# T5-bias attention with a mixture of adapters on one Trainium2 core: edge factors, last tokens' v and score tiles in another order

## The chip, the cores and the metric

The kernel runs on one core of one Trainium2 chip. The core has five engines with an instruction queue each: PE (TensorE, matrix multiply into PSUM), DVE (VectorE), ACT (ScalarE), POOL (GpSimd, which here works on SBUF alone) and SP (which issues nearly all DMAs). The metric is the device time of one execution in microseconds (us), the median of several runs. One execution was also recorded by the hardware profiler; the lines shown come from that one.

## The reference

Attention over 8 batches, 8 heads, 576 tokens and head size 64, with a bias that depends on the distance of two tokens (T5 buckets), then for each token the two best of 8 low-rank adapters are added:

```python
scores = q @ k.T / sqrt(D) + bias_table[bucket(|i - j|)]     # per batch and head
attn = softmax(scores);  x = attn @ v                        # x: 4608 tokens x 512
logits = x @ w_gate                                          # 8 experts, the top 2 per token
w = softmax of the top 2
out = x + sum over the top 2 of w * ((x @ A[e]) @ B[e])
```

All distances of 128 and more share one bucket, so only near pairs of tokens need a bias of their own.

## The kernel before, in words

A unit u is one batch and one pair of heads: 32 units, four for each batch. Tokens 0 to 511 of a batch are the main part, in four key tiles of 128 keys, and tokens 512 to 575 are the last tokens. All of the program is written out by hand in one order (`tc.manual_schedule()`); each engine executes its instructions in the order in which the Python code issues them, and waits on semaphores for the data and buffers that it needs.

For one unit, in the order of the main loop (`for u in range(2, NU - 2)`, before.py's main loop):

- `prep` lets POOL cast q and k of a later unit (L139); `load` issues DMAs on SP for unit u+4.
- `keys(u, c)` for three key tiles: PE writes scores of two heads, 128 keys by 512 queries, into a score tile (L436), adds the bias of near pairs by further matmuls (L441), and ACT takes the exp (L445). `KO` is the order of the four key tiles. In this text the first, second and third keys are these three calls, and the fourth comes further down.
- `step(u - 1, 0)`: the first values of the unit before. It may begin with `moe_d`, in which PE multiplies with the adapters' second factor (L627) and DVE adds x (L304) into an output tile, then PE multiplies probabilities with v (L524 for main keys, L532 for the last tokens' v as keys, L541 and L543 for the last tokens as queries) and, for a finished tile of x, with the gates and adapters' first factor (L571). DVE takes the reciprocal of the sums (L563), normalises (L564), copies z (L576) and its largest values (L577); when a group is complete, POOL does the gating's first four operations (L587 to L593).
- `edge_l(u)` on POOL (L505) and `edge_t(u)` on DVE (L510) multiply the edge probabilities of unit u with their bias factors, in place. An edge is a score between a last token and a main token. These probabilities are wanted by the values of unit u, one stage later.
- `prep_late` lets POOL cast v of unit u+1 (L135), and in some stages q and k of last tokens (L147).
- the fourth keys of u; then `turn`: PE transposes q and k of unit u+2 and tiles of x or gates into a score tile (L379, L377), and DVE copies it to SBUF (L381). In seven stages (`tcorner`: u = 4, 7, 11, 15, 19, 23, 27) the same tile also takes the corner scores of a batch, last tokens against last tokens, whose exp (L386) ACT takes only after the exp of the next unit's edges.
- `edges(u + 1)`: PE writes the edge scores of the next unit (L495, L498), ACT takes their exp (L500).
- `step(u - 1, 1)`: the second values of the unit before, with DVE's reciprocal, normalisation and, at times, z.
- in seven stages (`tv`) `cast_tail` casts the last tokens' v of a batch (L150): POOL the lower half, DVE the upper half. In some stages the gating's second part (`moe_w`), and behind corners POOL multiplies the corner probabilities with their factor (L484).

Score tiles, 128 partitions by two banks of PSUM, come from three pools in turn (`score_tile`). A stage uses six: first, second, third and fourth keys, the turned tile and the next unit's edges. So the second keys of u use the tile of the turned tile of u-1, the third keys that of the edges of u, and the edges of u+1 that of the third keys of u. A tile can be written again when its reader (ACT's exp or DVE's copy) is done. The values go to another pair of PSUM banks, which `moe_d` uses as well.

After the loop the last two units are done with keys in halves, and the last tiles' gates and adapters follow in banks that take the place of the score tiles (`fin`, with `s0` as the number of the pool that would be next).

Of the kernel before, what the change touches and what calls it, by code (L numbers as in the profile page):

```python
# [2 lines left out]

# [1 line left out]

# [22 lines left out]
def _ap(t, offset, dims):  # L28

    return bass.AP(tensor=t.tensor, offset=t.offset + offset, ap=[list(t.ap[0])] + dims)  # L30
# [8 lines left out]
def kernel(  # L39
# [12 lines left out]
    B, H, S, D = q.shape  # L52
# [26 lines left out]
    scx = ExitStack()  # L79
    scps = [scx.enter_context(tc.tile_pool(name=f"sc{i}_ps", bufs=1, space=bass.MemoryType.PSUM))  # L80
            for i in range(3)]
    turns = count()

    def score_tile(name, shape=(128, 2, SM), dt=FP32):
        return scps[next(turns) % 3].tile(list(shape), dt, name=name, tag="sc")

    KO = (0, 2, 1, 3)
    units = [(b, hp) for b in range(B) for hp in range(HP)]
# [42 lines left out]
    def cast(u, nm, eng):  # L131
        s = stage[(u, nm)].rearrange("p h (c d) -> p h c d", c=4)
        if nm == "v":
            t = vts[u % NV]
            eng.tensor_copy(t[:, :, :, :D].rearrange("p c h d -> p h c d"), s)  # L135
        else:
            t = qkp.tile([128, 4, 2, D], BF16, name=f"{nm}n", tag=f"{nm}n")
            copy = eng.copy if eng is nc.scalar else eng.tensor_copy
            copy(t.rearrange("p c h d -> p h c d"), s)  # L139
            nat[(u, nm)] = t  # L140

    def cast_tail(b, nm, eng, g0=0, g1=HP):
        if nm == "qk":
            if g0 == 0:
                nat[(b, nm)] = stt.tile([128, H, D], BF16, name="qkb", tag="qkb")
            part = slice(2 * g0, 2 * g1)
            eng.tensor_copy(nat[(b, nm)][:, part], tstage[(b, nm)][:, part])  # L147
            return
        for f, e in enumerate((eng, nc.vector)):
            e.tensor_copy(tvs[b % 2][f * 64:f * 64 + 64, :, f, :D], tstage[(b, nm)])  # L150
# [64 lines left out]
    def turned(h):  # L215
        return anti[h * 64:h * 64 + 64, 64 - 64 * h:128 - 64 * h]
# [122 lines left out]
    def tile_of(b, i):  # L339
        if (b, i) not in tiles:  # L340
            tiles[(b, i)] = tail_tile(b) if i == 4 else main_tile(b, i // 2, i % 2)
        return tiles[(b, i)]
# [87 lines left out]
    def keys(u, c):  # L430
        b, hp = units[u]
        qT, kT = qkT[u][:, 0, :], qkT[u][:, 1, :]
        sc = score_tile("sc")
        g, e = c // 2, c % 2
        for rows, prt, h, f in QUADS:
            nc.tensor.matmul(sc[prt, h, :],  # L436
                             lhsT=kT[rows, c * 128 + f * 64:c * 128 + f * 64 + 64],
                             rhs=qT[rows, :], start=True, stop=False, skip_group_check=True)
        for rows, prt, h, f in QUADS:
            p0, n, y0 = BAND[g][f]  # L440
            nc.tensor.matmul(_ap(sc[prt, h, :], p0, [[256, 2], [128, 2], [1, n]]), lhsT=turned(h),  # L441
                             rhs=_ap(Wt[rows, hp, :], 2 * y0 + (GP if e else 1),
                                     [[1, 2], [1 - GP if e else GP, 2], [2, n]]),
                             start=False, stop=True, skip_group_check=True)
        nc.scalar.activation(probs[u][0][:, c, :, :], sc, ACT.Exp, scale=scale)  # L445
# [61 lines left out]
    def edge_t(u, eng=nc.vector):  # L507
        hp = units[u][1]
        e = _ap(probs[u][1], 64 + 128, [[SM, 2], [1, 128]])
        eng.tensor_tensor(e, e, ET[:, hp], op=ALU.mult)  # L510
# [35 lines left out]
    def values(u, j):  # L546
        pv = mp.tile([128, 512], FP32, name="pv", tag="mm")
        pv_main(u, pv, j, range(4))
        pv_last(u, pv, j)
        pv_tail(u, pv, j)  # L550
        return pv
# [9 lines left out]
    def normalise(u, j, pv):  # L561
        b, hp, rc = outputs(u)
        nc.vector.reciprocal(rc[:, j, :5], _ap(pv, D, [[W1, 5]]))  # L563
        nc.vector.tensor_tensor(xs[b][:, j, hp], _ap(pv, 0, [[W1, 5], [1, D]]),  # L564
                                _ap(rc, 6 * j, [[1, 5], [0, D]]), op=ALU.mult)
# [3 lines left out]
    def moe_z(t, pv, o=ZO, cs=range(HP), first=False):  # L569
        for c in cs:  # L570
            nc.tensor.matmul(pv[:, o:o + ER + E], lhsT=t.xT[c], rhs=AW[:, c, :], start=first and c == cs[0],  # L571
                             stop=(c == HP - 1), skip_group_check=True)

    def moe_zc(t, pv, o=ZO):
        g, k = t.group, t.k
        nc.vector.tensor_copy(g.z[:, k, :], pv[:, o:o + ER + E])  # L576
        nc.vector.max(g.top[:, k, :], g.z[:, k, ER:])  # L577
        g.left -= 1
        if not g.left:
            moe_s(g)  # L580
# [28 lines left out]
    def moe_t(t, pv, o=ZO):  # L609
        ps = pv[:, o:o + 64].bitcast(BF16)  # L610
        nc.tensor.transpose(ps, t.group.zt[:, t.k, :, :].rearrange("p e r -> p (e r)"), ident)
        return ps

    def moe_tc(t, ps):
        t.zT = ms.tile([128, 128], BF16, name="zT", tag="zT", bufs=6)
        nc.vector.tensor_copy(t.zT, ps)
# [6 lines left out]
    def moe_d(t):  # L623
        dl = mp.tile([128, Dm], FP32, name="dl", tag="mm")
        if t.quarter:
            x_first(t, dl)
        nc.tensor.matmul(dl, lhsT=t.zT, rhs=Bc, start=not t.quarter, stop=True, skip_group_check=t.quarter)  # L627
        ot = ms.tile([128, Dm], FP32, name="ot", tag="ot", bufs=8)
        if t.quarter:
            nc.vector.tensor_copy(ot, dl)  # L630
        else:
            t.add(ot, dl)
        t.store(ot)

    def step(u, j, ds=(), z=None, zt=None):
        for t in ds:
            moe_d(tile_of(*t))
        pv = values(u, j)
        if z:
            moe_z(tile_of(*z), pv)  # L640
        if zt:
            ps = moe_t(tile_of(*zt), pv)
        normalise(u, j, pv)
        if z:
            moe_zc(tile_of(*z), pv)
        if zt:
            moe_tc(tile_of(*zt), ps)
# [90 lines left out]
    tturn = {3 if c == 1 else 6 if c == 2 else 4 * c - 4: c for c in range(1, B)}  # L738
    tload = {max(4 * c - 6, 3): c for c in range(2, B)}
    tq = {w - 1: c for w, c in tturn.items() if c != 2}  # L740
    tv = {4 if c == 1 else 6 if c == 2 else 4 * c - 3: c for c in range(1, B)}

    tcorner = {4 if c == 1 else 4 * c - 1: c for c in range(1, B)}
    pxs = {}

    def prep(u):
        for x in (u + 2, u + 3)[:1 + (u in wq)]:
            if x < NU and (x, "q") not in nat and x not in qkT:
                for nm in ("q", "k"):
                    cast(x, nm, nc.gpsimd)  # L750
        if u == 6:
            cast_tail(2, "qk", nc.gpsimd)

    def prep_late(u):
        if u + 1 < NU:
            cast(u + 1, "v", nc.gpsimd)
        if u in tq:
            cast_tail(tq[u], "qk", nc.gpsimd)

    za, zb, da, db, ta, tb, xt, wq = ({} for _ in range(8))  # L760
# [59 lines left out]
    for u in range(2, NU - 2):  # L820
        b, hp = units[u]
        prep(u)
        if u + 4 < NU:
            load(u + 4)
        if u == 2:
            load_tail(1, "v")
        if u in tload:
            load_tail(tload[u])
        for c in KO[u == 2:3]:
            keys(u, c)  # L830
        if u == 4:
            weights_turn(0)
        zs = za.pop(u, [None])
        step(u - 1, 0, da.pop(u, []), z=zs[0], zt=ta.pop(u, [None])[0])
        edge_l(u)
        edge_t(u)
        prep_late(u)
        if u == 3:
            weights_cast()
        keys(u, KO[3])  # L840
        if u == 4:
            weights_turn(1)
        items = []
        if u + 2 < NU:
            items.append(qk_item(u + 2))
        if u in tturn:
            items.append(tl_item(tturn[u]))
        for fn, bb, i in xt.pop(u, []):
            items.append(fn(tile_for(bb, i)))
        def next_edges():  # L850
            open_probs(u + 1)
            edges(u + 1)

        behind = u in tturn and tturn[u] == units[u + 1][0]
        turn(items, corner=tcorner.get(u), after=None if behind else next_edges)
        zs = zb.pop(u, [None])
        step(u - 1, 1, db.pop(u, []), z=zs[0], zt=tb.pop(u, [None])[0])
        if behind:
            next_edges()
        if u in tv:  # L860
            cast_tail(tv[u], "v", nc.gpsimd)
        for bb, i in wq.pop(u, []):
            moe_w(groups[(bb, i)])
        if u in tcorner:
            corners_bias(tcorner[u], pxs.pop(tcorner[u]))
# [104 lines left out]
    turn([x_item(T(L, 2), 0, 3), x_item(T(L, 3), 0, 3)])  # L970
    turned_gate(groups[(L - 1, 2)].zt, 2, ((L - 1, 2), (L - 1, 3)), act, "zta")

    s0 = next(turns)
    scx.close()
    fps = [ctx.enter_context(tc.tile_pool(name=f"fin{i}_ps", bufs=1, space=bass.MemoryType.PSUM))
           for i in range(3)]
# [106 lines left out]
```

## Time and profile before

| | |
|---|---|
| median of 3 runs | 192.33 us (190.65, 192.33, 193.86) |
| the profiled execution | 190.94 us |
| its span, first to last instruction | 189.1 us |
| granted TensorE clock, mean of the span | 0.991 |
| DMA | 39.40 MB, mean 208 GB/s |

The page gives busy times by engine. PE's busy share holds matmuls whose ends are modelled and which overlap, so it isn't a measure of how much PE could still do. In a timeline a row has the start (us from the span's start), the length (us), the engine, the line and operation, the tile written and read with their shapes, and how many instructions were merged (x4); in brackets stands the idle time in front and what ended it. The group rows have the mean length of one in ns; a row "a: min/median/max" gives ns as well.

### The profile page before, as it was taken

Reading aid. Unit: us, or ns where it says so; the run is one execution under the profiler, and the core shown is the slowest. Engines: PE = TensorE matmul, PEld = TensorE weight load, DVE = VectorE, ACT = ScalarE, POOL = GpSimd, SP = SyncE. Lnnn points to the kernel's source line nnn. Section 1 sums busy time; section 2 is a strip of 40 time slices with the busy share of each in tenths; the row PEclk is TensorE's granted clock in tenths of the full one; section 3 lists DMA queues with packets and bytes.
Section 4 is the critical chain, followed back from the end, with each engine's and each line's share of the span. In section 5 each row is a group of like instructions: output and inputs, shape, how many; then the busy total and the mean of one; then the engine's idle time right before and its main releaser. Section 6 shows DMA issues by size and latency. Waiting matters only on the chain.

```text
span 189.1 us, 9917 instructions
## 1 busy us (share of the span) xinstructions
PE 174.3 (92%) x4270; PEld 126.1 (67%) x4293; DVE 134.3 (71%) x344; ACT 164.4 (87%) x199; POOL 111.6 (59%) x250
## 2 busy tenths in 40 slices
PE   7796998999999999999999989999999999999980
PEld 2344675767767776766777667767777686788950
DVE  7626745576846876797778977787779788788770
ACT  3349998899999999998999998998999989987880
POOL 7444955468279835893189426972589538535230
PEclk9999999999999999999999999999999999999996
DMA  5899887899868788687977784798977844333346
GB/s 143 246 213 279 223 208 221 234 251 257 205 196 236 205 242 253 201 250 203 264 228 221 184 244 135 231 290 229 254 213 229 241 138 116 112 118 98 128 159 231
DMA packets 63667, 39.40 MB, mean 208 GB/s; under 512 B 17408, under 2 KB 58888, under 8 KB 63624
## 3 DMA queue, kind: packets, MB, share of 16 engines
q1 hardware_dynamic: 63000, 38.38, 71.6%
q8 instruction: 33, 0.54, 1.3%
q10 hardware_dynamic: 624, 0.39, 0.8%
q14 instruction: 10, 0.08, 0.2%
HBM read 29.31 MB, written 9.45 MB: 205 GB/s over the span
## 4 chain that ended last, share of the span: by engine, by line
PE 72%; ACT 11%; DVE 7%; issue 3%; DMA 2%; POOL 1%; SPq 1%; ACTq 0%; DVEq 0%; POOLq 0%
PE pv L524 16%; PE sc L436 15%; ACT pk L445 8%; PE tx L379 7%; PE sc L441 7%; PE pv L571 4%; PE sc L498 3%; PE pv L541 3%; PE pv L532 3%; PE sc L495 3%; ACT pt L500 2%; PE busy L659 2%; DMA qkt<-in_k_dram 2%; DVE tx L381 2%; PE dl L627 1%
## 5 line engine op out<-in xcount | busy, mean ns | idle before, releaser
L445 ACT ACTIVATE pk<-sc 128x1024 bf16<-128x1024 f32 x120 | 113.5, 1030 | 6.9 <-PE sc L441 6.5
L436 PE MATMUL sc<-tx 64*64 64x512 bf16 x480 | 47.5, 389 | 1.8 <-DVE tx L381 0.6
L524 PE MATMUL pv<-v,pk 128*128 128x65 bf16 x992 | 41.4, 193 | 2.9 <-PE sc L441 2.7
L524 PEld LDWEIGHTS <-pk 128*128 128x128 bf16 x1024 | 37.6, 97 | 9.3 <-issue 2.1
L441 PE MATMUL sc<-Wt,anti 64*64 64x256 bf16 (+1 forms) x480 | 41.4, 306 | 0.0
L381 DVE COPY tx<-tx 128x2048 bf16<-128x2048 bf16 (+7 forms) x34 | 34.7, 1021 | 3.7 <-PE tx L379 3.7
L500 ACT ACTIVATE pt<-sc 128x1024 bf16<-128x1024 f32 x32 | 33.4, 1043 | 3.7 <-PE sc L498 2.1
L564 DVE TENSOR_TENSOR xn<-pv,rc 128x320 bf16<-128x320 f32 x62 | 30.5, 491 | 2.1
L563 DVE RECIPROCAL rc<-pv 128x5 f32<-128x5 f32 x62 | 11.8, 191 | 20.4 <-PE pv L571 14.9
L436 PEld LDWEIGHTS <-tx 64*64 64x64 bf16 x480 | 17.1, 104 | 13.8 <-issue 4.5
L304 DVE TENSOR_TENSOR ot<-dl,xn 128x512 f32<-128x512 f32 x25 | 17.3, 690 | 12.7 <-PE sc L441 9.1
L505 POOL TENSOR_TENSOR pt<-pt,EL 128x128 bf16<-128x128 bf16 x32 | 13.6, 427 | 17.8 <-ACT pt L500 9.5
L135 POOL CAST v<-vs 128x512 bf16<-128x512 f32 x32 | 20.0, 627 | 4.0 <-PE pv L543 2.2
L139 POOL CAST qn<-qs 128x512 bf16<-128x512 f32 x30 | 19.2, 640 | 1.7 <-DMA qs<-in_q_dram 1.7
L139 POOL CAST kn<-ks 128x512 bf16<-128x512 f32 x29 | 18.0, 620 | 0.4 <-DMA ks<-in_k_dram 0.4
L541 PE MATMUL pv<-v,pt 128*128 128x65 bf16 x248 | 17.8, 194 | 0.0
L484 POOL TENSOR_TENSOR pc<-pcx,EC 128x256 bf16<-128x256 bf16 x8 | 5.5, 684 | 20.4 <-ACT pcx L386 19.9
L532 PE MATMUL pv<-vb,pt 128*128 128x130 bf16 x124 | 17.4, 223 | 0.0
L441 PEld LDWEIGHTS <-anti 64*64 64x64 bf16 x480 | 16.0, 106 | 0.2
L541 PEld LDWEIGHTS <-pt 128*128 128x128 bf16 x256 | 14.1, 98 | 0.1
L379 PEld LDWEIGHTS <-qn 64*128 64x128 bf16 x256 | 5.6, 94 | 10.5 <-issue 6.9
L571 PE MATMUL pv<-AW,tx 128*128 128x136 bf16 x124 | 12.5, 224 | 0.0
(149 smaller groups left out, 283.4 us busy)
## 6 DMA issues: line engine op xcount, KB each, us to landing
qs<-in_q_dram SPq DMA_DIRECT2D x32, 256.0 KB, 4.3
vs<-in_v_dram SPq DMA_DIRECT2D x64, 128.0 KB, 3.8
out_dram<-ot SPq DMA_DIRECT2D x32, 256.0 KB, 3.1
ks<-in_k_dram SPq DMA_DIRECT2D x62, 128.0 KB, 4.2
vt<-in_v_dram SPq DMA_DIRECT2D x8, 128.0 KB, 4.3
qkt<-in_q_dram SPq DMA_DIRECT2D x7, 128.0 KB, 4.2
qkt<-in_k_dram SPq DMA_DIRECT2D x7, 128.0 KB, 3.6
out_dram<-ot SPq DMA_DIRECT2D x7, 128.0 KB, 2.5
```

The source lines that it names most:

```text
L135: eng.tensor_copy(t[:, :, :, :D].rearrange("p c h d -> p h c d"), s)
L139: copy(t.rearrange("p c h d -> p h c d"), s)
L381: copy(sb[:, :n], ps.rearrange("p a (c i) -> p c a i", i=64)[:, :n])
L436: nc.tensor.matmul(sc[prt, h, :], lhsT=kT[rows, c * 128 + f * 64:c * 128 + f * 64 + 64], rhs=qT[rows, :], start=True, stop=False, skip_gro ...
L441: nc.tensor.matmul(_ap(sc[prt, h, :], p0, [[256, 2], [128, 2], [1, n]]), lhsT=turned(h), rhs=_ap(Wt[rows, hp, :], 2 * y0 + (GP if e else 1 ...
L445: nc.scalar.activation(probs[u][0][:, c, :, :], sc, ACT.Exp, scale=scale)
L500: nc.scalar.activation(probs[u][1][:, 64:], sc.rearrange("p h x -> p (h x)"), ACT.Exp, scale=scale)
L524: nc.tensor.matmul(pv[:, o:o + W1], lhsT=pk_slice(u, c, h, j + 2 * f), rhs=vm[:, c, h, :], start=first, stop=False, skip_group_check=True)
L532: nc.tensor.matmul(_ap(pv, h * W1, [[130, 2], [1, W1]]), lhsT=probs[u][1][:, x0:x0 + 128], rhs=tvs[b % 2][:, 2 * hp + h].rearrange("p f d ...
L541: nc.tensor.matmul(pv[:, o:o + W1], lhsT=probs[u][1][:, x0:x0 + 128], rhs=vts[u % NV][:, c, h, :], start=False, stop=False, skip_group_che ...
L564: nc.vector.tensor_tensor(xs[b][:, j, hp], _ap(pv, 0, [[W1, 5], [1, D]]), _ap(rc, 6 * j, [[1, 5], [0, D]]), op=ALU.mult)
L571: nc.tensor.matmul(pv[:, o:o + ER + E], lhsT=t.xT[c], rhs=AW[:, c, :], start=first and c == cs[0], stop=(c == HP - 1), skip_group_check=True)
```

## The change

Three things, each in the code that issues the instructions:

1. In the main loop `edge_l(u)` and `edge_t(u)` are issued ahead of `step(u - 1, 0, ...)` instead of behind it.
2. `tv`, the stages at whose end the last tokens' v is cast: for batches 3 to 7 it is 4c - 2 instead of 4c - 3, so u = 10, 14, 18, 22, 26 instead of 9, 13, 17, 21, 25. Batches 1 and 2 keep u = 4 and 6.
3. The pool of the next score tile comes from a list, `ring`, that is rotated. In the stage behind one with corner scores (u = 5, 8, 12, 16, 20, 24, 28) the first two entries are exchanged after the first keys, so the second keys take the tile of the edges and the third keys the turned tile of the stage before, and the three tiles then go on in turn in that order. `s0` is the list's next entry.

```diff
-    turns = count()
+    ring = [0, 1, 2]
 
     def score_tile(name, shape=(128, 2, SM), dt=FP32):
-        return scps[next(turns) % 3].tile(list(shape), dt, name=name, tag="sc")
+        ring.append(ring.pop(0))
+        return scps[ring[-1]].tile(list(shape), dt, name=name, tag="sc")
...
-    tv = {4 if c == 1 else 6 if c == 2 else 4 * c - 3: c for c in range(1, B)}
+    tv = {4 if c == 1 else 4 * c - 2: c for c in range(1, B)}
...
         for c in KO[u == 2:3]:
             keys(u, c)
+            if c == KO[0] and u - 1 in tcorner:
+                ring[:2] = ring[1::-1]
         if u == 4:
             weights_turn(0)
         zs = za.pop(u, [None])
-        step(u - 1, 0, da.pop(u, []), z=zs[0], zt=ta.pop(u, [None])[0])
         edge_l(u)
         edge_t(u)
+        step(u - 1, 0, da.pop(u, []), z=zs[0], zt=ta.pop(u, [None])[0])
         prep_late(u)
...
-    s0 = next(turns)
+    s0 = ring[0]
```

More of the change, by code (lines that the diff above doesn't have):

```diff
@@ L1 @@
 from contextlib import ExitStack
-from itertools import count
 import numpy as np
```

## The prediction

> **What bounds the kernel now.** I read the page first (engines, costliest groups), then the ACT timeline of the main loop, then PE's and DVE's timelines around each stage that is longer than the others, last the sources of the moved lines. A stage here is one u of the loop; I time it from the first exp of u to the first exp of u+1, which are the ACT rows "x4" of L445.
>
> ```profile
> PE 174.3 (92%) x4270; PEld 126.1 (67%) x4293; DVE 134.3 (71%) x344; ACT 164.4 (87%) x199; POOL 111.6 (59%) x250
> ...
> L445 ACT ACTIVATE pk<-sc 128x1024 bf16<-128x1024 f32 x120 | 113.5, 1030 | 6.9 <-PE sc L441 6.5
> ```
> ```profile
> 71.80 1.05 ACT L500 ACTIVATE pt<-sc 128x1024 bf16<-128x1024 f32 x1
> 72.70 0.43 ACT L386 ACTIVATE pcx<-tx 128x256 bf16<-128x256 f32 x1
> 73.09 3.92 ACT L445 ACTIVATE pk<-sc 128x1024 bf16<-128x1024 f32 x4
> ...
> 78.35 3.77 ACT L445 ACTIVATE pk<-sc 128x1024 bf16<-128x1024 f32 x4 [0.24 <-PE sc L441]
> ...
> 83.27 3.82 ACT L445 ACTIVATE pk<-sc 128x1024 bf16<-128x1024 f32 x4 [0.24 <-PE sc L441]
> ...
> 88.66 3.77 ACT L445 ACTIVATE pk<-sc 128x1024 bf16<-128x1024 f32 x4 [0.37 <-PE sc L441]
> ...
> 93.83 3.77 ACT L445 ACTIVATE pk<-sc 128x1024 bf16<-128x1024 f32 x4 [0.20 <-PE sc L441]
> ...
> 98.84 3.77 ACT L445 ACTIVATE pk<-sc 128x1024 bf16<-128x1024 f32 x4 [0.21 <-PE sc L441]
> ...
> 103.77 3.77 ACT L445 ACTIVATE pk<-sc 128x1024 bf16<-128x1024 f32 x4 [0.24 <-PE sc L441]
> ...
> 108.69 3.02 ACT L445 ACTIVATE pk<-sc 128x1024 bf16<-128x1024 f32 x3 [0.23 <-PE sc L441]
> ...
> 114.76 3.77 ACT L445 ACTIVATE pk<-sc 128x1024 bf16<-128x1024 f32 x4 [0.53 <-PE sc L441]
> ...
> 124.61 3.77 ACT L445 ACTIVATE pk<-sc 128x1024 bf16<-128x1024 f32 x4 [0.24 <-PE sc L441]
> ...
> 129.94 3.77 ACT L445 ACTIVATE pk<-sc 128x1024 bf16<-128x1024 f32 x4 [0.37 <-PE sc L441]
> ```
> ```profile
> 101.75 0.29 PE L495 MATMUL sc<-tx 64*128 64x64 bf16 x8
> ```
> The bare stage is 98.84 to 103.77, 4.93 us, and it is a ring through two engines. Four exps of 1.03 us in 3.77 us start 0.91 us apart, so the third ends at 98.84 + 2 x 0.91 + 1.03 = 101.7. It frees the score tile of the edges; PE begins those at 101.75 (L495), goes on through the second values and the first keys of the next u, and the exp of these starts at 103.77. ACT has some 0.2 us idle in each stage, PE next to none. DVE and POOL have slack on the mean, so they matter only where PE finds a score tile not yet given back. The rows above are u = 12 (73.09), 13, 14, 15, 16, 17, 18, 19 (108.69), 20, then 22 and 23. Stages over 4.93: u=12 takes 5.26, u=14 5.39, u=16 5.01, u=19 6.07, u=22 5.33.
>
> **Where PE finds a tile late.** The second keys (L436) of u take the tile that held the turned tile of u-1. They must wait for DVE's copy of it (L381) and, behind a corner, for the corner exp too (L386).
>
> ```profile
> 72.40 0.41 PE L436 MATMUL sc<-tx 64*64 64x512 bf16 x4
> ...
> 73.18 0.41 PE L436 MATMUL sc<-tx 64*64 64x512 bf16 x4 [0.19 <-ACT pcx L386]
> ...
> 73.55 0.42 PE L436 MATMUL sc<-tx 64*64 64x512 bf16 x4
> ```
> ```profile
> 93.14 0.41 PE L436 MATMUL sc<-tx 64*64 64x512 bf16 x4
> ...
> 93.68 0.41 PE L436 MATMUL sc<-tx 64*64 64x512 bf16 x4
> ```
> ```profile
> 82.58 0.41 PE L436 MATMUL sc<-tx 64*64 64x512 bf16 x4
> ...
> 83.24 0.41 PE L436 MATMUL sc<-tx 64*64 64x512 bf16 x4
> ```
> ```profile
> 108.01 0.41 PE L436 MATMUL sc<-tx 64*64 64x512 bf16 x4
> ...
> 109.15 0.41 PE L436 MATMUL sc<-tx 64*64 64x512 bf16 x4 [0.56 <-DVE tx L381]
> ```
> ```profile
> 123.92 0.41 PE L436 MATMUL sc<-tx 64*64 64x512 bf16 x4
> ...
> 124.53 0.41 PE L436 MATMUL sc<-tx 64*64 64x512 bf16 x4
> ```
> Two keys follow each other in 0.37 us when nothing waits (73.18 to 73.55). So the second keys are late by 0.41 us at u=12 and 0.17 at u=16 (both behind corners), 0.29 at u=14, 0.77 at u=19 and 0.24 at u=22. A late start is worth no more than what the stage is over 4.93.
>
> **Part 1, edge factors ahead of the values.** Nothing is added or removed: per stage of the loop one L510 on DVE and one L505 on POOL move in front of the first values' reciprocal and normalisation. PE, ACT and SP keep their order.
>
> ```profile
> 29.64 0.30 PE L379 MATMUL tx<-ident,qkb 64*128 64x64 bf16 x8
> ```
> ```profile
> 29.59 0.72 DVE L510 TENSOR_TENSOR pt<-pt,ET 128x256 bf16<-128x256 bf16 x1
> 30.23 0.94 DVE L381 COPY tx<-tx 128x1536 bf16<-128x1536 bf16 x1
> ...
> 79.33 0.69 DVE L304 TENSOR_TENSOR ot<-dl,xn 128x512 f32<-128x512 f32 x1 [0.80 <-PE sc L441]
> 80.34 0.20 DVE L563 RECIPROCAL rc<-pv 128x5 f32<-128x5 f32 x1 [0.31 <-PE pv L571]
> ...
> 81.39 0.67 DVE L510 TENSOR_TENSOR pt<-pt,ET 128x256 bf16<-128x256 bf16 x1
> 81.98 1.21 DVE L381 COPY tx<-tx 128x2048 bf16<-128x2048 bf16 x1
> ...
> 104.08 2.14 DVE L150 CAST vb<-vt 64x512 bf16<-64x512 f32 x1
> ...
> 108.08 1.02 DVE L381 COPY tx<-tx 128x1664 bf16<-128x1664 bf16 x1
> ...
> 122.72 0.61 DVE L510 TENSOR_TENSOR pt<-pt,ET 128x256 bf16<-128x256 bf16 x1
> ```
> ```profile
> L510 DVE TENSOR_TENSOR pt<-pt,ET x32: 270/274/737, 19.2 to 171.4; 128x256 bf16<-128x256 bf16 x32
> ```
> ```profile
> L150 DVE CAST vb<-vt x8: 423/612/2136, 17.2 to 145.4; 64x512 bf16<-64x512 f32 x8
> ```
> At u=13 the factor sits directly before the copy and takes 0.67 instead of 0.27; the copy starts 0.59 later for it (81.39 to 81.98), ends at 83.19, and the second keys of u=14 start at 83.24. With the factor gone from there the copy is 0.59 earlier, more than the 0.29 of lateness, and the stage is 0.46 over 4.93: gain 0.29. The same for u=22 (the factor of 0.61 again sits before the copy, 0.24 late, stage 0.40 over): gain 0.24. At u=3 the edges wait for the copy that ends at 31.17; its last transposes end at 29.94, and the copy starts at 30.23: with a little for the handover, 0.25 of these 0.29. The moved factor itself goes where DVE waits for PE (0.80 us before L304, another 0.31 before L563), so its 0.27 costs nothing. If it meets a long run of POOL work, the next thing late is L304, then the reciprocal, then the copy; queued behind it are just these. Elsewhere the copy comes 0.2 us earlier to tiles that are not late: nothing. On POOL the four small gating operations stand 0.43 us later behind L505, in a place where POOL waits for DVE's result and L505 has its input already: nothing, at most 0.4 us of gating that is wanted a stage later.
>
> **Part 2, the last tokens' v a stage later.** For five batches both halves of L150 (POOL and DVE) go from the end of u = 9, 13, 17, 21, 25 to the end of u+1. At u=17 the DVE half took 2.14 us, all that follows it came late, the copy ended at 109.10 and the second keys of u=19 began at 109.15. Without it the whole 0.77 is free; the stage is 1.14 over: gain 0.77. In the new place the copy behind it belongs to a corner's tile, which the corner exp holds longer anyway, and the 0.80 us before L304 cover a median cast of 0.61 (bounds 0.42 and 2.14). No DMA moves, and its staging buffer is wanted again only stages later: nothing.
>
> **Part 3, tiles exchanged behind a corner.** Behind seven corners the second keys take the edges' tile, free when L500 ends (71.80 + 1.05 = 72.85), and the third keys the tile that the corner exp frees (72.70 + 0.43 = 73.13). At u=12 the second keys can go at 72.90, the third at 73.27 instead of 73.55: 0.28 gained of 0.41, under the stage's 0.33 excess. At u=16 the lateness is 0.17, the excess 0.08: 0.08. I price u=8 and u=24, of the same build, like u=16 (estimate), and the other three corners at nothing. At the end of the kernel the tiles' order is reversed; a matmul group there waits for a copy that the next group needs anyway: nothing, at most a few matmuls.
>
> **Sum.** Part 1: 0.29 + 0.24 + 0.25 = 0.78. Part 2: 0.77. Part 3: 0.28 + 3 x 0.08 = 0.52. Together 2.07 us. Against it stands one risk that I price inside the forecast: the cast at 104.08 shows that DVE can sit through a run of POOL casts. If the factor does so at one stage, it ends where that cast ended, and the copy comes 0.2 earlier than at u=18, so 0.58 of lateness instead of 0.77; at even odds 0.3. Net 1.8. The profiled execution took 190.94 us (span 189.1 and 1.84 around it), so it would take 189.1. It lies 1.4 below the median of the three runs (192.33); the middle of all four, (190.94 + 192.33)/2 = 191.6, is what I start from: 189.8.
>
> The Trainium skill has a rule against this change ("SBUF — State Buffer", section "SBUF: two separate sides"): VectorE, when it has two SBUF inputs or runs a two-port mode, and GpSimd hold a shared port pair exclusively, and the loser blocks for a whole instruction. Row L510 agrees (0.27 alone, 0.74 at most); by that rule alone a factor pays no more than one POOL instruction, the 0.80 us cover it, and the sum would be the full 2.07, 189.5 us. The 2.14 of row L150 is longer than one POOL instruction, so I keep the 0.3.
>
> **The rivals.**
> ```profile
> 75.49 0.62 POOL L139 CAST kn<-ks 128x512 bf16<-128x512 f32 x1
> ```
> (a) Slower: the factor, now early in the stage, loses to POOL's whole run each time. Behind a corner that run lasts to 76.11; L304, which starts 0.98 after the stage's first exp (79.33 against 78.35), so near 74.1 there, would start at 76.4, 2.3 late; 0.31 of that is idle before the reciprocal and 0.2 is what the factor no longer takes, which leaves 1.8 for PE: five such stages cost up to 9, and five like u=18 0.58 each. With the gains gone: 191.6 + 9 + 2.9 = 203.5. It decides from three or four lost runs on, where the 2.07 are eaten. For it: 104.08. Against: the median cast of 0.61 got in after one POOL instruction.
> (b) No change: other waits take the place of those removed, because ACT's exps, the third keys waiting for the corner exp, or the gating work fill the stage; one of the three parts survives: 191.6 - 0.5 = 191.1. For it: ACT idles only 0.2 us a stage.
> (c) More: the runs spread over 3.2 us (190.65 to 193.86); if the slower ones hold more collisions like that at 104.08, taking them away is worth two more: 188.
>
> **How the numbers follow.** Forecast 0.50 (its own range 188.8 to 190.8), (b) 0.25, (c) 0.13, (a) 0.12. 2% is 3.8 us, about what a measurement of this kernel can tell from no change. Under 188.5 lies most of (c) and a little of the forecast's spread: 0.16. Over 196.2 most of (a): 0.09. Within: 0.75. The range from 187.7 to 192.5 holds the forecast, (b) and most of (c), and a single lost run of (a).
>
> **What would show it.** Right: second keys at u=14, 19, 22 within 0.4 us of the first; L150 on DVE under 0.8; behind corners no L386 wait on PE; the bare stage still 4.93; L510 of 0.3 to 0.7 in what was idle before L304. Wrong: L510 or L150 of 1.5 or more at several stages with L304 late behind it, or stages that stay long with the waits on L500 instead.

## The result and the profile after

| | before | after |
|---|---|---|
| median of 6 runs | 192.41 us (190.65 to 193.86) | 189.89 us (189.17 to 190.81) |
| ratio after / before, 95% interval | | 0.9897 [0.9848, 0.9946] |
| the profiled execution | 190.94 us | 189.71 us |
| its span | 189.1 us | 187.9 us |
| first exp of u=3 to first exp of u=29 | 133.56 us | 131.97 us |

The kernel is faster by about 1%: half of the 2% that the prediction took as the bound of "no change", but with an interval that lies wholly below 1. The ratio is that of the means, 189.98 over 191.96 us, without the run of 193.86 us, which lies over 1.5% above the fastest of its kernel.

The main loop lost 1.59 us. The rows that carry it are the same that the prediction showed. First the page of the kernel after: engines, and groups as busy time, mean ns of one, idle before.

```profile
PE 176.9 (94%) x4293; PEld 126.9 (68%) x4293; DVE 136.5 (73%) x344; ACT 163.8 (87%) x199; POOL 113.3 (60%) x250
...
L445 ACT ACTIVATE pk<-sc 128x1024 bf16<-128x1024 f32 x120 | 113.1, 1030 | 6.2 <-PE sc L441 5.6
...
L510 DVE TENSOR_TENSOR pt<-pt,ET 128x256 bf16<-128x256 bf16 x32 | 13.1, 413 | 0.3
```

Shares say little here: DVE and POOL are even a little busier than before, and the kernel is faster. What counts is when a stage's first exp starts. The ACT timeline of the kernel after:

```profile
73.11 3.77 ACT L445 ACTIVATE pk<-sc 128x1024 bf16<-128x1024 f32 x4
...
78.08 3.77 ACT L445 ACTIVATE pk<-sc 128x1024 bf16<-128x1024 f32 x4 [0.18 <-PE sc L441]
83.01 3.77 ACT L445 ACTIVATE pk<-sc 128x1024 bf16<-128x1024 f32 x4 [0.24 <-PE sc L441]
88.14 3.77 ACT L445 ACTIVATE pk<-sc 128x1024 bf16<-128x1024 f32 x4 [0.42 <-PE sc L441]
...
93.30 3.77 ACT L445 ACTIVATE pk<-sc 128x1024 bf16<-128x1024 f32 x4 [0.20 <-PE sc L441]
...
98.22 3.77 ACT L445 ACTIVATE pk<-sc 128x1024 bf16<-128x1024 f32 x4
...
108.08 3.77 ACT L445 ACTIVATE pk<-sc 128x1024 bf16<-128x1024 f32 x4 [0.24 <-PE sc L441]
...
113.43 3.77 ACT L445 ACTIVATE pk<-sc 128x1024 bf16<-128x1024 f32 x4 [0.39 <-PE sc L441]
...
123.29 3.77 ACT L445 ACTIVATE pk<-sc 128x1024 bf16<-128x1024 f32 x4 [0.24 <-PE sc L441]
128.68 3.77 ACT L445 ACTIVATE pk<-sc 128x1024 bf16<-128x1024 f32 x4 [0.42 <-PE sc L441]
```

These are u = 12, 13, 14, 15, 16, 17, 19, 20, 22 and 23; the differences of starts are the stages. The stages that changed, in us, before and after (the bare stage is 4.93; "again" is a second profile of the kernel after, told below):

| u | 3 | 8 | 12 | 14 | 16 | 19 | 22 | 24 | 25 |
|---|---|---|---|---|---|---|---|---|---|
| before | 5.36 | 5.05 | 5.26 | 5.39 | 5.01 | 6.06 | 5.33 | 5.02 | 4.93 |
| after | 5.11 | 4.93 | 4.98 | 5.12 | 4.92 | 5.36 | 5.39 | 4.93 | 5.07 |
| after, again | 5.20 | 4.93 | 4.98 | 5.12 | 4.92 | 5.36 | 5.12 | 4.93 | 4.93 |

All others agree within 0.07. Six of these are longer than 4.93 in every kernel and were not touched: u=4 (5.70), 15 and 23 (5.16), 26 (5.18), 27 (5.60) and 28 (5.14). Why the stages of the table are shorter is in the distance from the first to the second keys. PE's timeline of the kernel after, at u = 12, 14, 19 and 22:

```profile
72.42 0.41 PE L436 MATMUL sc<-tx 64*64 64x512 bf16 x4
...
72.92 0.41 PE L436 MATMUL sc<-tx 64*64 64x512 bf16 x4
...
82.32 0.41 PE L436 MATMUL sc<-tx 64*64 64x512 bf16 x4
...
82.68 0.44 PE L436 MATMUL sc<-tx 64*64 64x512 bf16 x4
...
107.39 0.41 PE L436 MATMUL sc<-tx 64*64 64x512 bf16 x4
...
107.75 0.44 PE L436 MATMUL sc<-tx 64*64 64x512 bf16 x4
...
122.60 0.41 PE L436 MATMUL sc<-tx 64*64 64x512 bf16 x4
...
122.97 0.44 PE L436 MATMUL sc<-tx 64*64 64x512 bf16 x4
```

0.50, 0.36, 0.36 and 0.37 us, where before it was 0.78, 0.66, 1.14 and 0.61. No row of the second keys carries a wait for L386 or L381 any more. The stage of u=22 is long all the same, for another reason. In the kernel after, the transposes at its end took 0.59 us for the 16 that took 0.32 in its second profile, and no wait is recorded:

```profile
126.14 0.59 PE L377 MATMUL tx<-ident,xn 64*64 64x64 bf16 x16
```
```profile
126.12 0.32 PE L377 MATMUL tx<-ident,xn 64*64 64x64 bf16 x16
```

The moved work sits where it was meant to. DVE's timeline of the kernel after, a factor and a cast in their new places:

```profile
123.35 0.36 DVE L510 TENSOR_TENSOR pt<-pt,ET 128x256 bf16<-128x256 bf16 x1
124.28 0.69 DVE L304 TENSOR_TENSOR ot<-dl,xn 128x512 f32<-128x512 f32 x1 [0.57 <-PE dl L627]
...
128.86 0.76 DVE L150 CAST vb<-vt 64x512 bf16<-64x512 f32 x1
```

The factor comes right behind the normalisation and DVE still waits 0.57 us for PE before L304: it fills idle time. The longest cast on DVE is 0.76 in this profile; before it was 2.14.

The two profiled executions differ by only 1.23 us, less than the loop, because this profile of the kernel after entered the loop later. The first exp of u=3, before and then after:

```profile
27.42 2.86 ACT L445 ACTIVATE pk<-sc 128x1024 bf16<-128x1024 f32 x3 [0.18 <-PE sc L441]
```
```profile
27.80 2.86 ACT L445 ACTIVATE pk<-sc 128x1024 bf16<-128x1024 f32 x3 [0.19 <-PE sc L441]
```

So profiles are compared below by the loop (u=3 to u=29), and kernels by the ratio of their repeated runs.

### The profile page after: what moved, and what is told of

Read it like the earlier page. It is cut to its first block, busy times and chain, and to the rows that moved or that the text cites. A ratio compares the mean times of both kernels' runs of the same rounds, so it can differ in the third digit from the quotient of the medians.

```text
span 187.9 us, 9941 instructions
## 1 busy us (share of the span) xinstructions
PE 176.9 (94%) x4293; PEld 126.9 (68%) x4293; DVE 136.5 (73%) x344; ACT 163.8 (87%) x199; POOL 113.3 (60%) x250
## 4 chain that ended last, share of the span: by engine, by line
PE 74%; ACT 9%; SPq 5%; DMA 4%; issue 2%; DVE 2%; POOL 1%; ACTq 0%; POOLq 0%
PE pv L524 15%; PE sc L436 14%; ACT pk L445 8%; PE tx L379 7%; PE sc L441 7%; PE dl L627 5%; PE sc L498 4%; PE pv L571 3%; PE pv L541 3%; PE pv L532 3%; PE sc L495 3%; DMA vs<-in_v_dram 2%; DMA ks<-in_k_dram 2%; SPq L109 2%; PE busy L659 2%
## 5 line engine op out<-in xcount | busy, mean ns | idle before, releaser
L381 DVE COPY tx<-tx 128x2048 bf16<-128x2048 bf16 (+7 forms) x34 | 34.9, 1026 | 4.8 <-PE tx L379 4.0
L505 POOL TENSOR_TENSOR pt<-pt,EL 128x128 bf16<-128x128 bf16 x32 | 13.8, 430 | 19.1 <-ACT pt L500 11.6
L436 PEld LDWEIGHTS <-tx 64*64 64x64 bf16 x480 | 16.4, 104 | 10.7 <-issue 1.8
L304 DVE TENSOR_TENSOR ot<-dl,xn 128x512 f32<-128x512 f32 x25 | 17.2, 689 | 8.5 <-PE dl L627 8.5
L135 POOL CAST v<-vs 128x512 bf16<-128x512 f32 x32 | 20.9, 654 | 4.0 <-PE pv L543 2.2
L510 DVE TENSOR_TENSOR pt<-pt,ET 128x256 bf16<-128x256 bf16 x32 | 13.1, 413 | 0.3
```

Of the source, the lines that this page charges most:

```text
L381: copy(sb[:, :n], ps.rearrange("p a (c i) -> p c a i", i=64)[:, :n])
L436: nc.tensor.matmul(sc[prt, h, :], lhsT=kT[rows, c * 128 + f * 64:c * 128 + f * 64 + 64], rhs=qT[rows, :], start=True, stop=False, skip_gro ...
```

## The experiments

The theory: three independent causes of late second keys, one taken away by each part, on a ring of 4.93 us that stays. The first rival is that the collisions with POOL only move or were chance; the second is that the ring is set elsewhere.

**Part 1 alone**, on the kernel before:

```diff
-        step(u - 1, 0, da.pop(u, []), z=zs[0], zt=ta.pop(u, [None])[0])
         edge_l(u)
         edge_t(u)
+        step(u - 1, 0, da.pop(u, []), z=zs[0], zt=ta.pop(u, [None])[0])
```

> The kernel before with part 1 alone (edge factors ahead of the first values). Late-tile theory: second keys at u=14 and u=22 within 0.4 us of the first, the edges at u=3 some 0.25 us earlier, so 0.5 to 0.8 us off the loop; u=19 keeps its lateness only if the cast of the last tokens' v is held up again. Ratio 0.996. Rival (no change, the waits only move): ratio 0.999 to 1.001 and stages u=14 and u=22 as long as before. Rival (POOL's runs hold the factor up): L510 of 1.5 us or more at several stages, ratio over 1.

Measured: 190.73 us, ratio 0.9953 [0.9925, 0.9981]; loop 132.12, 1.44 less where 0.5 to 0.8 was expected. u = 3, 14 and 22 became 5.11, 5.12 and 5.12, and the stages behind corners stayed. But u=19 fell to 5.36 too, although the cast was not moved. POOL's and DVE's timelines of this kernel, at the place of the 2.14 us cast:

```profile
103.66 0.43 POOL L505 TENSOR_TENSOR pt<-pt,EL 128x128 bf16<-128x128 bf16 x1 [0.17 <-ACT pt L500]
104.03 0.86 POOL L135 CAST v<-vs 128x512 bf16<-128x512 f32 x1
```
```profile
104.00 0.42 DVE L150 CAST vb<-vt 64x512 bf16<-64x512 f32 x1
```

Here the cast got in at once, and it was POOL's next cast that was drawn out (0.86). So part 1 by itself also takes what the prediction gave to part 2.

**Part 2 alone**, on the kernel before:

```diff
-    tv = {4 if c == 1 else 6 if c == 2 else 4 * c - 3: c for c in range(1, B)}
+    tv = {4 if c == 1 else 4 * c - 2: c for c in range(1, B)}
```

> The kernel before with part 2 alone (last tokens' v cast a stage later). Late-tile theory: no cast over 0.8 us on DVE in the new place or, if one is, no late tile behind it; u=19 without its 0.77 us; u=14 and u=22 still late, since the edge factor still sits before the copy (though POOL's half of the cast no longer collides with it there, so L510 may be short and the lateness smaller). Ratio 0.996, and a smaller spread between the runs if the slower runs of before hold such collisions. Rival (no change): ratio 0.999 to 1.001, spread as before.

Measured: 190.53 us, 0.9962 [0.9931, 0.9992]; loop 132.56, 1.0 less. u=19 5.36; u=14 (5.37) and u=22 (5.31) stayed late. u=3 was 5.11 without any edit there: that factor met no POOL cast this time. The DVE casts are 0.42 to 0.81 us.

**Part 3 alone**, on the kernel before:

```diff
+            if c == KO[0] and u - 1 in tcorner:
+                ring[:2] = ring[1::-1]
```

> The kernel before with part 3 alone (two score tiles exchanged behind corners). Late-tile theory: second keys of u = 5, 8, 12, 16, 24 within 0.5 us of the first; stages u=8, 12, 16, 24 shorter by 0.1, 0.3, 0.1, 0.1 us; the rest as before; ratio 0.997. Rival (the third keys wait for the corner exp instead): third keys late by as much as the second were, stages unchanged, ratio 1.

Measured: 191.64 us, 1.0002 [0.9971, 1.0034]; loop 132.89, 0.67 less. Stages 8, 12, 16 and 24 are 4.93, 4.98, 4.92 and 4.93, and u = 14, 19, 22 stayed at 5.41, 6.03, 5.34, with the long cast again. The stages are as expected; in time nothing can be told from no change, and the expected 0.997 lies just below the interval.

**The kernel before, again**, one execution with its profile: is the 2.14 us cast chance?

> The kernel before once more, to see which of its late tiles are there each time. If the late tiles come from the order of the work, u=12, 14, 16, 22, 24 are late again by the same amounts to 0.1 us. The cast of 2.14 us at u=17 depends on who gets there first, so it may be gone, or stand at another u of 9, 13, 17, 21, 25.

Measured: 190.88 us, loop 133.53. The late stages came again to 0.03 us (u=14 5.38, u=19 6.06, u=22 5.33), and the row of all casts by DVE too, as min/median/max ns:

```profile
L150 DVE CAST vb<-vt x8: 422/570/2136, 17.1 to 145.3; 64x512 bf16<-64x512 f32 x8
```

The collision belongs to the order of the program and not to the one execution.

**The casts put into POOL's corner run**, on the kernel after: here rival (a) should show. Batch 2 stays at u=6 in this edit, so the casts that move are those to u = 11, 15, 19, 23 and 27.

```diff
-    tv = {4 if c == 1 else 4 * c - 2: c for c in range(1, B)}
+    tv = {4 if c == 1 else 6 if c == 2 else 4 * c - 1: c for c in range(1, B)}
```

> The changed kernel with the last tokens' v of batches 2 to 7 cast one stage later again (u = 7, 11, 15, 19, 23, 27), so that DVE's half meets POOL's run behind a corner: corner factors and then four casts with nothing between. Rival (a) of the prediction, that DVE sits through a whole run: casts of 2 us or more at several of these stages, the first values' reciprocal late and the second or third keys late by 0.5 us or more; ratio to before near or over 1. Theory that DVE gets in at the first POOL instruction's end and sat through a run only by an unlucky offset: casts of 0.4 to 1.0 us, no late tile, ratio as for the changed kernel, 0.99.

Measured: 190.87 us, 0.9952 [0.9912, 0.9992], where the second theory expected 0.99; loop 132.43. No cast sat through the run (0.42 to 0.90 us), and no second keys came late. Yet u=16 and u=24 took 5.33 us instead of 4.92. DVE's and PE's timelines of this kernel in u=16:

```profile
94.91 0.80 DVE L150 CAST vb<-vt 64x512 bf16<-64x512 f32 x1
95.74 0.58 DVE L510 TENSOR_TENSOR pt<-pt,ET 128x256 bf16<-128x256 bf16 x1
96.25 0.68 DVE L304 TENSOR_TENSOR ot<-dl,xn 128x512 f32<-128x512 f32 x1
96.85 0.18 DVE L563 RECIPROCAL rc<-pv 128x5 f32<-128x5 f32 x1
97.06 0.49 DVE L564 TENSOR_TENSOR xn<-pv,rc 128x320 bf16<-128x320 f32 x1
```
```profile
97.61 0.20 PE L379 MATMUL tx<-ident,xn 64*128 64x64 bf16 x2 [0.29 <-DVE xn L564]
97.65 0.28 PE L495 MATMUL sc<-tx 64*128 64x64 bf16 x8
```

Cast and factor, 0.80 and 0.58, use up all idle time before L304; the normalisation behind it is late, and PE waits 0.29 us for its result in the transposes that stand before the edges (L495), which are in the ring. This is the cover that the prediction named, and its end: one drawn-out cast and one drawn-out factor together are more than it holds.

**Both halves of the cast on POOL** (batches 3 to 7), on the kernel before; the cast does not move, only leaves DVE.

```diff
-        for f, e in enumerate((eng, nc.vector)):
+        for f, e in enumerate((eng, nc.vector if b < 3 else eng)):
```

> The kernel before, with both halves of the last tokens' v of batches 3 to 7 cast by POOL at the old places, so DVE has no cast there. If the 0.77 us at u=19 come from DVE's cast sitting through POOL's run, they are gone without anything being moved: stage u=19 at 5.4 us, u=14 and u=22 late as before or more (POOL's second half now lies under the factor too), ratio 0.996. If they come from the place (the end of u=17 is crowded), u=19 stays at 6.0 us and the ratio at 1.00.

Measured: 191.28 us, 0.9982 [0.9957, 1.0008]; loop 132.81, 0.75 less. u=19 is 5.36, u=14 stays at 5.37 and u=22 at 5.45, of which 0.13 is a pause within its transposes (L377, 0.45 us instead of 0.32). So what had made u=19 late was DVE's cast and nothing else near it. The ratio does not decide: its interval holds the expected 0.996 as well as 1.

**The next edges before the turned tile**, on the kernel after, without the exchange; another way to give the second keys a free tile.

```diff
-            if c == KO[0] and u - 1 in tcorner:
-                ring[:2] = ring[1::-1]
...
-        turn(items, corner=tcorner.get(u), after=None if behind else next_edges)
+        if not behind:
+            next_edges()
+        turn(items, corner=tcorner.get(u))
```

> The changed kernel without the exchange, but with the edges of the next unit issued ahead of the turned tile on PE in every stage of the loop (not at u=3). In turn, the second keys then take the edges' tile and the third keys the turned tile everywhere. Late-tile theory: corners behave as with the exchange (second keys within 0.5 us), the bare stage stays 4.9 us, since the turned tile now waits for the third exp where the edges did; ratio as for the changed kernel, 0.990, to 0.002. Rival: DVE's copy starts 0.45 us later in each stage, its second reciprocal with it, and PE waits for the bank of the values: stages 0.1 to 0.3 us longer, ratio 1.00 to 1.03.

Measured: 193.72 us, 1.0085 [1.0049, 1.0122], slower than before; the expected gain was missed. Loop 134.52. Second keys behind corners were on time, but most bare stages took 5.03 to 5.05 us. Ratio and stages are what the rival expected, so its mechanism has to be looked for as well. Its timelines, ACT and then PE:

```profile
99.55 3.77 ACT L445 ACTIVATE pk<-sc 128x1024 bf16<-128x1024 f32 x4 [0.24 <-PE sc L441]
...
104.60 1.02 ACT L445 ACTIVATE pk<-sc 128x1024 bf16<-128x1024 f32 x1 [0.36 <-PE sc L441]
```
```profile
101.95 0.29 PE L495 MATMUL sc<-tx 64*128 64x64 bf16 x8
...
102.46 0.29 PE L379 MATMUL tx<-ident,qn 64*128 64x64 bf16 x8
...
103.03 0.67 PE L524 MATMUL pv<-v,pk 128*128 128x65 bf16 x16
```

The third exp ends at 99.55 + 2 x 0.91 + 1.03 = 102.4, and now the turned tile waits for it (102.46). From there to the values it is 0.57 us; from the edges to the values it was 0.46 in the kernel after, here in u=17:

```profile
101.13 0.29 PE L495 MATMUL sc<-tx 64*128 64x64 bf16 x8
...
101.59 0.67 PE L524 MATMUL pv<-v,pk 128*128 128x65 bf16 x16
```

The ring grew by this 0.11 in the stages whose turned tile holds 32 transposes. With 24 of them (u = 5 and 10) the stage stayed at 4.93 and 4.92, and at u=15, where the corner scores stand there too, it went from 5.16 to 5.41. The rival's wait of PE for the bank of the values is not needed for this: the turned tile starts 0.05 us behind the third exp in each of these bare stages, as the edges did in the kernel after. So the ring is what the prediction took it for: whatever stands between the third exp and the next first keys is paid in every stage.

The same explains stages that are long in every kernel. PE's timeline of the kernel after has more work behind the edges at u=15 (the adapters' first factor) and at u=19 (a `moe_d`); both stand there before the change too:

```profile
91.04 0.29 PE L495 MATMUL sc<-tx 64*128 64x64 bf16 x8
...
92.28 0.40 PE L571 MATMUL pv<-AW,tx 128*128 128x136 bf16 x4
...
111.44 0.40 PE L620 MATMUL dl<-ident,tx 128*128 128x128 bf16 x4
111.67 0.38 PE L627 MATMUL dl<-Bc,tx 128*128 128x512 bf16 x1
```

They are what is left over 4.93 there: 0.23 us at u=15 and 0.43 at u=19.

**The kernel after, again**, beside the experiments:

> The changed kernel again, beside the others on the same chip. Ratio 0.990; late tiles only at u=8 and u=12 (second keys 0.5 us behind the first); the pause of 0.28 us in the middle of one group of transposes at u=22, where no wait was recorded, gone or at another place if it is an accident of one execution.

Measured: 190.12 us (before 191.92), 0.9906 [0.9869, 0.9943]; loop 131.72, 1.84 less than before. The pause of u=22 is gone and u=25 is back at 4.93, so both were accidents of one execution. One cast took 1.36 us at the end of u=6 (48.60, behind the next stage's first exp at 48.43): POOL had waited for a DMA of k and was late, and DVE sat through L505 and a cast. The next stage stayed at 4.92, so the risk of a cast sitting through POOL work is still there, but here it fell where there was slack.

**Parts 1 and 2 without the exchange**, twice. The profiled execution of the first took 383.25 us, with PE busy for 368.0 of them, and tells nothing of the stages; its other ten took 189.71 to 191.68. The second has a profile that can be used:

> The changed kernel without the exchange of tiles (parts 1 and 2). Late-tile theory: stages u = 8, 12, 16, 24 are 0.12, 0.28, 0.09, 0.09 us longer than in the changed kernel, all others as there: ratio 0.993 where the changed kernel has 0.990. Rival (part 3 is worth nothing in the time, as it measured alone): the same ratio as the changed kernel.

> The changed kernel without the exchange of tiles once more, for its trace. Late-tile theory: stages u = 8, 12, 16, 24 of 5.05, 5.26, 5.01, 5.02 us where the changed kernel has 4.93, 4.98, 4.92, 4.93, the rest as there: 0.58 us in the loop, a ratio 0.003 above the changed kernel's. Rival: the stages as in the changed kernel.

```diff
-            if c == KO[0] and u - 1 in tcorner:
-                ring[:2] = ring[1::-1]
```

Measured: 190.42 us, 0.9917 [0.9886, 0.9948], and 190.48 us, 0.9923 [0.9883, 0.9962]; loop 132.14. u = 8, 12, 16, 24 are back at 5.06, 5.26, 5.01, 5.02, together 0.59 more than in the kernel after. Both ratios are above those of the kernel after (0.9897, 0.9906) by 0.001 to 0.003, the right way, but well within the intervals; 0.003 was expected. Here too a cast at the end of u=6 took 1.22 us at no cost (u=6 and 7 of 4.92). The exchange is worth 0.6 us in the trace; in time its worth is not resolved.

**Parts 2 and 3 without the edges ahead**, on the kernel after:

```diff
+        step(u - 1, 0, da.pop(u, []), z=zs[0], zt=ta.pop(u, [None])[0])
         edge_l(u)
         edge_t(u)
-        step(u - 1, 0, da.pop(u, []), z=zs[0], zt=ta.pop(u, [None])[0])
```

> The changed kernel without part 1 (parts 2 and 3). Late-tile theory: u=14 and u=22 late again by 0.25 us each, u=19 free, corners as in the changed kernel; loop 0.5 us longer than the changed kernel's, ratio 0.993 to 0.994. If part 1 is worth the 0.9 us that it measured alone, the ratio is 0.995.

Measured: 190.79 us, 0.992 [0.9889, 0.9952]; loop 132.55. The corner stages 12, 16 and 24 and u=19 are as in the kernel after (u=8 is not, 5.23: PE waited 0.27 us there for POOL's cast of k, queued behind a cast whose DMA came late); the second keys of u=14 (stage 5.54) and u=22 (5.30) are late again, by 0.15 and 0.20. Of the 0.61 that u=14 is over 4.93, part is the same pause as above, not lateness: its 16 transposes (L377) took 0.60 instead of 0.32.

**Only DVE's factor ahead**, on the kernel before; POOL's stays. Which half of part 1 freed the cast in the first experiment?

```diff
+        edge_t(u)
         step(u - 1, 0, da.pop(u, []), z=zs[0], zt=ta.pop(u, [None])[0])
         edge_l(u)
-        edge_t(u)
```

> The kernel before with DVE's edge factor alone ahead of the first values, POOL's behind as it was. u=14 and u=22 are no longer late. With all of part 1 the cast at u=17 took 0.42 us where it took 2.14 before. If that is because POOL then waits for the edges' exp and starts L505 earlier than DVE's cast by 0.33 us, the cast takes 2.1 us again here and u=19 is late by 0.7: ratio 0.998. If it is because DVE is earlier, the cast takes under 0.8 us and the ratio is 0.995, as with all of part 1.

Measured: 191.51 us, 0.9976 [0.9946, 1.0005]. u=14 and u=22 are 5.12 and 5.11, so these are DVE's half. But u=19 is 6.03 again, as the first of the two readings expected:

```profile
104.35 0.42 POOL L505 TENSOR_TENSOR pt<-pt,EL 128x128 bf16<-128x128 bf16 x1
104.72 0.61 POOL L135 CAST v<-vs 128x512 bf16<-128x512 f32 x1
105.28 0.61 POOL L139 CAST qn<-qs 128x512 bf16<-128x512 f32 x1
105.83 0.61 POOL L139 CAST kn<-ks 128x512 bf16<-128x512 f32 x1
```
```profile
104.46 2.27 DVE L150 CAST vb<-vt 64x512 bf16<-64x512 f32 x1
```

POOL's casts run back to back at full speed, and DVE's single cast ends 0.3 us behind the last of them. Both kernels have DVE's factor ahead; what differs is POOL's. So POOL's half was needed to free the cast: with it POOL had caught up with ACT (in the first experiment L505 waits 0.17 us for the exp) and met the cast at another moment. POOL's half alone was not run.

## Why the prediction was right, point by point

**The ring and the bare stage.** Right. Bare stages are 4.92 to 4.93 in all kernels that leave PE's order alone, and 5.03 to 5.05 in the one that lengthened the ring by 0.11. The list of stages over 4.93 was not complete: its own rows give u=15 as 93.83 - 88.66 = 5.17. That stage is long by work in the ring, which no part touches, so nothing in the sum hangs on it.

**Part 1.** The price was 0.29 + 0.24 + 0.25 = 0.78. Measured, before to after, again: u=14 0.27, u=22 0.21, u=3 0.16 (0.25 in the first profile), together 0.64 to 0.73. The step "the copy comes earlier, and a late start is worth no more than the stage's excess" holds, and "the moved factor costs nothing" too: its mean rose to 413 ns, in idle time. The third term is the weak one. Up to u=8 the program of part 2 alone is that of before, and u=3 took 5.11 there, 5.21 with both halves of the cast on POOL, and 5.36 and 5.33 in the two profiles of before: without part 1 it is chance how much of the factor lies under a POOL cast (L510 of 0.72 us in before, 0.28 with part 2 alone). With part 1 it took 5.11 or 5.12 in six of seven profiles. So the worth of this term is 0 to 0.25, by execution.

**Part 2.** The price 0.77, measured 0.70 (6.06 to 5.36). The size is right, the attribution was too narrow. The prediction read the 2.14 us cast as a matter of its place. The runs show a matter of phase against POOL: the same 0.70 comes by moving the cast, by taking DVE out of it, or by part 1 with both its halves (one profile), and not by DVE's factor alone. Where POOL's factor was priced ("nothing, at most 0.4 us of gating"), this gain was overlooked. As each of these two parts brings it, the parts do not add up: alone they took 1.44, 1.0 and 0.67 us from the loop, 3.1 in all, together 1.6 to 1.8.

**Part 3.** The price 0.28 + 3 x 0.08 = 0.52, measured 0.28 (u=12) + 0.12 + 0.09 + 0.09 = 0.58. Pricing u=8 like u=16 was 0.04 low. In time this is below what these runs resolve.

**The risk of 0.3.** It was priced for a factor that sits through a POOL run; none did. The longest L510 in the kernel after is 0.70 us, and 0.71 in its second profile. What is missing from the full 2.07 is 0.07 at u=19 and a few hundredths at u=14 and 22, and accidents elsewhere: the pause of 0.28 at u=22 and 0.14 at u=25 in the first profile, 0.09 at u=3 and 0.06 at u=6 in the second. So the net of 1.8 came out as 1.59 and 1.84 by another road than the one it was argued by: what was lost were accidents, and that they came near the 0.3 is luck.

**The rule of the Trainium skill** that the prediction set against the change ("SBUF — State Buffer", section "SBUF: two separate sides": the loser of the shared port pair blocks for a whole instruction) fits the factors, which paid at most 0.53 us over their 0.27 (0.80, with the next edges before the turned tile), less than one POOL cast of 0.61. For the casts the 2.14 to 2.27 us rows disagree with one instruction as the bound: there the loser waited through L505 and three POOL casts, in each of four executions with POOL's factor at its old place and this cast on DVE at u=17 (before twice, part 3 alone, only DVE's factor ahead).

**Start and sum.** 191.6 less 1.8 gave 189.8; measured 189.89. The start was a choice: the median of before came out as 192.41 beside the first runs of after, and as 191.1, 191.92 and 191.9 beside the three groups of experiments. From the ratios, 192.41 x (1 - 0.9897) = 2.0 and 191.92 x (1 - 0.9906) = 1.8 us; the interval of the first reaches from 1.0 to 2.9. The agreement to 0.1 us is better than the measurement supports; it is luck.

**The rivals.** (a) fell: in its new place no factor took over 0.80 us and no cast over 0.90, not even when the casts were put into the corner run. What did cost there was the path that (a) named, a late L304 and all behind it, at 0.41 us in each of two stages. (b) fell: the waits taken away did not come back on other tiles, and both intervals of the kernel after end below the 0.997 that its 191.1 us stand for. (c), that slower runs of before hold more collisions, was not shown: the second profile of before has the same ones. The runs of after spread less (1.6 against 3.2 us, and 2.2 against 3.1 in the second comparison, there with 10 runs against 32), but no profile caught a run of before over 191, and the start-up alone moves by 1.4 us between profiles (below), so it stays open.

## What to carry to other kernels

Find the ring that sets a stage's bare length first, and then price an edit only by what the single stages are over that length: summing those excesses gave 2.07 us where the loop lost 1.59 to 1.84, while busy shares pointed nowhere. When a wait comes from two engines in each other's way, ask what else would shift their phase before crediting the gain to one edit, and run each part alone, since parts that free the same wait do not add up. For effects of 1% compare a stretch of the trace that starts behind the kernel's start-up, and let repeated runs give the ratio.

## What the runs showed of the hardware

- **Who sits through whom.** DVE's cast (0.42 us alone) and POOL's casts (0.61) collide in two ways. In all 29 cases of these profiles in which the DVE cast started 0.31 to 0.34 us behind POOL's L505 it took 0.42, and where a POOL cast came next, that one was drawn out (0.86 in the rows of part 1 alone: 104.00 against 103.66). Started 0.24 us behind L505 in the kernel before, or 0.11 behind it with only DVE's factor ahead (104.46 against 104.35), with three POOL casts following without a gap, it took 2.14 and 2.27 and POOL lost nothing. So 0.1 us in the start went with 1.7 us in the length; why POOL's back-to-back instructions let the waiting one in only at their end was not tried.
- **The start-up moves by over 1 us from one execution to the next.** The first exp of u=3 came between 27.37 (before, again) and 28.78 us (casts in the corner run). In the latter a part of it fits TensorE's clock. Its four warming matmuls took nearly twice the time of those of the kernel before, here before and then that kernel:

```profile
6.44 1.04 PE L659 MATMUL busy<-A 128*128 128x512 bf16 x4
```
```profile
6.54 1.89 PE L659 MATMUL busy<-A 128*128 128x512 bf16 x4
```

  The Trainium skill says why that can differ ("TensorE: Matmul & The Clock Gate", section "What's actually happening"): the clock is halved until a window of activity is over, and the window runs freely, not from the kernel's start. The rows agree with a late end of the halved clock in that execution. Two other late starts have the short rows here, but a low clock later: with both halves of the cast on POOL (28.55) and without the edges ahead (28.39) the granted clock from 15.0 to 18.5 us was 0.52, where the kernel before has 1.00. The late start with only DVE's factor ahead (28.45) has neither, so not all of the spread is explained.
- **Pauses of 0.28 us within PE's transposes.** The 16 of L377 took 0.59 and 0.60 instead of 0.32 in two executions, at different u, with no wait for another engine recorded and no instruction longer than usual; in a third they took 0.45. A pause of 0.28 is as large as what part 1 gained at u=14.
